# Block-sparse attention and a residual MLP on one core: the first head's keys prepared in two pieces

## The chip, the core and the metric

The kernel runs on one core of a Trainium2 chip. The core has five engines with instruction queues of their own, which work side by side and wait for each other through semaphores: PE (TensorE, matrix products; its weight loads are listed as PEld), DVE (VectorE), ACT (ScalarE), POOL (GpSimd) and SP (SyncE). The last two mainly issue transfers (DMA) here. PE reads the on-chip memory and writes to PSUM, eight banks of 512 float32 values per partition; DVE and ACT read PSUM and write back to the on-chip memory, which has 128 partitions.

The metric is device microseconds of one launch. The kernel before takes 306.7 us (median of six runs, 305.7 to 308.58).

## The reference

Two stages are chained. The first is attention with a block mask, for 4 batches, 8 heads, 768 positions and 64 numbers per head:

```python
scores = scale * np.matmul(q, k.transpose(0, 1, 3, 2))
mask = np.abs(blk_i - blk_j) <= window          # 24 blocks of 32 positions
mask = mask | (blk_i == 0) | (blk_j == 0) | (blk_i == n_blocks - 1) | (blk_j == n_blocks - 1)
for qb in range(n_blocks):
    for kb in sampled_blocks[qb]:               # 3 sampled blocks per row of blocks
        mask[qb*block:(qb+1)*block, kb*block:(kb+1)*block] = True
scores = np.where(mask, scores, -1000000000.0)
attn = softmax(scores)
x = matmul(attn, v)                             # then (batch, seq, 512)
```

The second stage is a residual MLP that also mixes positions:

```python
a1 = alpha1 * x + beta1
u = x + lam * np.einsum('ts,bsd->btd', w_tok, a1)
a2 = alpha2 * u + beta2
out = u + lam * (np.maximum(a2 @ w_ch1, 0.0) @ w_ch2)
```

## The kernel before

**Units.** The 32 heads are worked in 16 pairs (4 batches of 4 pairs). Each pair needs 9 units of 1024 score columns, so there are 144 units. A unit is: scores on PE (L922 for the first six pairs, L941 after them) into a PSUM tile `sps` or into two banks `gb`; an exponential on ACT (L960) into a buffer `eT`; and products with v on PE (L984). A column of ones beside v in `vext` gives the sum of the row, by which DVE divides (L1000, L1003). For the first six pairs the mask is part of the score product: the transposed keys carry 24 more rows that say to which block a position belongs, the queries 24 rows with -400 where a block is masked. For later pairs DVE multiplies by a mask (L965).

**Getting q and k into place.** The score product needs q and k with the head's numbers on the partitions. For the first six pairs PE transposes 128x128 tiles against an identity (L425), three of q and three of k per head, and DVE or ACT copies the result out of PSUM into `qk` (L481), 64 partitions at a time, so there are two copies (r = 0 and 1) per transposed bank. Later pairs use transposing DMAs on SP's queue (L818, L841) and two copying DMAs (L862).

**The MLP.** Per pair or two pairs, DVE makes `a1p` (L1156, L1167), PE multiplies by the transposed token weights `wtokT` (L1205), DVE adds into `x_sb` (L1229) and makes `ub` (L1243). Per half batch follow 16 products with the first channel weights (L1352) with a ReLU on ACT or DVE (L1391, L1399), and the second channel weights (L1432) with the final sum (L1454) and the output DMA (L1473).

**What sets the order.** Two parts. A hand-written start, up to L458, puts the first instructions on each engine in program order. It is the part that the change edits: on SP's queue the load of the first head's q (`q2f`, L360), three loads of the block rows, the second head's q (L365); on ACT's queue the sampled blocks (L359) and the two heads of k (`k2f`, L361, L364); on POOL counters, then loads. DVE builds the mask rows and the identity, PE makes two small products (L430) that say which blocks are masked, ACT and DVE cast q and k to bf16 (`first_cast`, into `relp`), PE transposes three tiles of each, and DVE copies q's, ACT k's. `keep_warm` issues products of constants into a bank that nobody reads.

After it comes a planner, `Plan`. Every later instruction group is an operation with the engines that may run it, an estimated duration, a due time, the operations that it depends on, and the PSUM banks or buffers that it needs. `Plan.run` steps through an estimated time and gives each engine that is free the ready operation with the earliest due time, so the order on every engine, and whether DVE or ACT makes a copy, come out of these estimates; it is written down as program order. Three of its inputs are touched by the change: the estimated time at which each engine is free after the start (the second dictionary given to `Plan`, L463), the estimated landing of the second head's q and k (L892), and `SEEDS` (L48). For each seed a part of the due times within a stretch of the schedule is shifted at random, with the same outcome in each build. Twenty-four single constant products (`fill`, L686) have the latest due times of all, so they stand wherever the planner sees PE with nothing else to do, and the rest of them at the end.

The loads of q, k, v and weights go out on POOL's queue, in an order that the planner also sets. With eight semaphores, a load waits for the one eight places before it.

Of the kernel before, what the change touches and what calls it, by code (L numbers as in the profile page):

```python
# [24 lines left out]
D = 64  # L25
# [5 lines left out]
P = 128  # L31
NT = S // P
HS = S // 2
# [11 lines left out]
EXPB = -0.35667494  # L45
T0 = 6
FINE = 3
SEEDS = [3340310007, 3340310011, 3340310015, 3340310024, 3340310026, 3340310027, 3340310065, 3340310070, 3340310081, 3340310120, 3340310138, 3340310152, 3340310166, 3340310177, 3340310178, 3340310179, 3340310340, 3340310371, 3340310405, 3340310518, 3340310537, 3340310574, 3340310590, 3340310686, 3340310729, 1340310788, 1340310806, 1340310822, 1340310954, 1340310957, 3340311162, 3340311192, 3340311406, 3340311549, 3340312202, 3340312526, 3340312534, 1340312821, 1340312995, 2340313211, 2340313318, 1340313338, 3340313793, 1340314038, 1340314057, 1340314590, 1340315664, 3340316245, 1363480032, 1363480039, 3363480372, 3363480518, 1363480765, 4363481891, 4363482185, 4363482912, 4363483188]  # L48
NFILL = 24
ORD = ((0, 2, 4, 1, 3, 5), (1, 3, 5, 0, 2, 4))  # L50
HF = 3 * S
# [222 lines left out]
def kernel(  # L274
# [17 lines left out]
    nc = tc.nc  # L292
# [21 lines left out]
    qkr = [t[0:D].rearrange("p w h (g r t) -> p w h g r t", g=3, r=2) for t in qk2]  # L314
# [17 lines left out]
    relp = pp.tile([P, 2, 2, NT * D], BF, name="relp", tag="relp")  # L332
# [18 lines left out]
    gbT = [ps.tile([P, 512], FP, name=f"gb{i}", tag=f"gb{i}") for i in range(4)]  # L351
# [6 lines left out]
    k2f = wk.tile([P, 2, NT * D], FP, name="k2f", tag="hts", bufs=2)  # L358
# [33 lines left out]
    def keep_warm(n, w, to=gbT[3]):  # L392
        for _ in range(n):
            nc.tensor.matmul(to[:, 0:w], ones[:, 0:P], ones[:, 0:w], start=True, stop=True)  # L394

    keep_warm(6, 512)

    def where(out, what, op, lim):
        nc.vector.tensor_single_scalar(out, cnt[what][0].bitcast(U16), float(lim), op=op)
# [8 lines left out]
        out=eqt[MB, :, 0:NR],  # L408
# [5 lines left out]
        out=mbb[MB, :], in_=eqt[MB], axis=mybir.AxisListType.X, op=ALU.max  # L414
# [3 lines left out]
    def first_cast(a, i, eng):  # L418
        src = (q2f, k2f)[i]
        eng(out=relp[:, a, i, :], in_=src[:, a, :])  # L420

    def transposes(bank, src, slots=range(NT)):
        tps = bank.bitcast(BF)[:, 0 : NT * P].rearrange("p (o c) -> p o c", o=NT)
        for o in slots:
            nc.tensor.transpose(tps[:, o, :], src(o), identb[:])  # L425
        return tps

    bq_ps = (spsT[1], gbT[2])
    for w in (0, 1):
# [4 lines left out]
            start=True,  # L434
            stop=True,
        )
    first_cast(0, 1, nc.scalar.copy)
    first_cast(0, 0, nc.vector.tensor_copy)
    nc.scalar.activation(
        qx2[0][MB, 0, HS:S], bq_ps[1][0:NBLK, 0:HS], AF.Copy, bias=-BIG, scale=BIG  # L440
# [2 lines left out]
        out=qx2[0][MB, 0, 0:HS],  # L443
# [3 lines left out]
        op0=ALU.mult,  # L447
        op1=ALU.subtract,
    )
    keep_warm(2, P)  # L450
    for w in range(2):
        t = transposes(gbT[w][:], lambda o: relp[:, 0, w, ts(o, P)], range(3))
        for r in range(2):
            cp = nc.scalar.copy if w else nc.vector.tensor_copy
            cp(out=qkr[0][:, w, 0, :, r, :], in_=t[r * D : (r + 1) * D, 0:3])
    keep_warm(10, P)
    for t in vext:
        nc.vector.memset(t[:, :, :, D:VW], 1.0)  # L458


    pl = Plan(
        dict(sps=2, gb=4, eT=NE, q=4, k=4, v=4, vx=3, qk=2, hts=2, a1p=2, ub=2, ot=2),
        dict(PE=5800, ACT=6050, DVE=5800, POOL=4000, SP=4000),  # L463
    )
    GB = [("gb", 0), ("sps", 0)]
    GL = [("gb", 0), ("sps", 0)]
# [71 lines left out]
    def landed(name, t):  # L538
        op = Op(name, [], 0, None)
        op.start, op.vis = 0, t  # L540
        return op
# [88 lines left out]
    for g in range(4):  # L630
# [6 lines left out]
                deps=[x.tr for x in WTT],  # L637
# [31 lines left out]
        deps=[BC["lam"]],  # L669
# [216 lines left out]
    for i in range(2):  # L886
        op = pl.dve(
            ("fc", i),
            dve(384, 2),
            1 + 0.1 * i,  # L890
            lambda op, i=i: first_cast(1, i, nc.vector.tensor_copy),
            deps=[landed(("f", i), 5600 - 500 * i)],  # L892
        )
        FC1.append(op)
    ROWS = []
# [630 lines left out]
```

## Time and profile before

The profiled execution took 306.59 us, of which 304.8 us are the span from the first to the last instruction.

| what | us | where it is from |
|---|---|---|
| profiled execution | 306.59 | times |
| its span | 304.8 | page |
| PE busy | 297.8 (98%) | page, part 1 |
| DVE busy | 232.4 (76%) | page, part 1 |
| ACT busy | 177.4 (58%) | page, part 1 |
| first k, first head landed, cast on ACT begins | 4.45 | order of time, ACT |
| first score product | 6.01 | order of time, PE |
| first exponential | 6.83 | order of time, ACT |
| first product with v | 10.07 | order of time, PE |
| first use of the token weights | 28.36 | order of time, PE |

How to read it: a row in order of time gives the start and the duration in us, the engine, the line, the operation, what it writes and reads with shapes and types, how often it stands in a row, and in brackets how long the engine was idle before it and what ended that. A row of windows gives, for each stretch, its length, the busy time of PE, PEld, DVE, ACT and POOL with the number of instructions, the granted PE clock, the share of the DMA engines in use and what they moved. Products on PE are pipelined: a 512-wide one lasts 0.38 us in the record, but the next starts 0.22 us after it, so pace is read from the distance of the starts. Busy shares over the whole span hide stages: ACT is over nine tenths busy between 10 and 30 us and idle in the last 50.

### The profile page before, as it was taken

What the parts mean: (1) busy time and instruction counts of PE and PEld (TensorE: products, weight loads), DVE (VectorE), ACT (ScalarE), POOL (GpSimd) and SP (SyncE); (2) the same over time, 40 slices, a digit from 0 to 9 for tenths busy, and PEclk for the clock granted to TensorE, in tenths of its full rate; (3) what the DMA queues carried; (4) which work ended last, traced back from release to release, by engine and by line L of the source; (5) the groups of instructions that cost most, each with busy time, mean ns of one, the idle gap of its engine ahead of it and who ended that gap; (6) DMA issues with size and microseconds to landing.
All of it is one profiled execution on the core that took longest, in us unless ns stands there. A gap on an engine that the chain in (4) does not pass through costs nothing.

```text
span 304.8 us, 7147 instructions
## 1 busy us (share of the span) xinstructions
PE 297.8 (98%) x2967; PEld 186.3 (61%) x2996; DVE 232.4 (76%) x438; ACT 177.4 (58%) x242; POOL 44.6 (15%) x71
## 2 busy tenths in 40 slices
PE   7899999999999999999999999999999999999997
PEld 2677888765674566555756565555665574555545
DVE  5669989999799699858977986878778763856532
ACT  5898799988597765768577454767567520000000
POOL 9466252304010102110000000000000000000000
DMA  7999999999967726945161225123030005000011
GB/s 146 205 251 200 206 205 206 199 153 135 180 109 117 131 54 93 178 85 115 38 115 39 76 62 103 38 62 87 2 86 37 0 2 150 8 34 34 37 65 72
DMA packets 50672, 31.38 MB, mean 103 GB/s; under 512 B 27784, under 2 KB 47056, under 8 KB 50640
## 3 DMA queue, kind: packets, MB, share of 16 engines
q0 software_dynamic: 17520, 15.47, 33.4%
q1 hardware_dynamic: 32796, 15.06, 21.8%
q8 instruction: 23, 0.38, 0.5%
q10 hardware_dynamic: 324, 0.39, 0.4%
q14 instruction: 9, 0.07, 0.1%
HBM read 30.78 MB, written 6.29 MB: 122 GB/s over the span
## 4 chain that ended last, share of the span: by engine, by line
PE 90%; ACT 5%; DMA 2%; issue 2%; DVE 1%; SPq 0%; ACTq 0%
PE gb L1352 27%; PE gb L1432 27%; PE gb L984 11%; PE gb L1205 10%; PE sps L922 5%; ACT eT L960 4%; PE sps L941 4%; PE gb L941 3%; DMA q2f<-in_q_dram 2%; PE gb L425 1%; PE sps L1205 0%; SPq L363 0%; PE gb L394 0%; DVE qk L899 0%; ACT wtokT L479 0%
## 5 line engine op out<-in xcount | busy, mean ns | idle before, releaser
L960 ACT ACTIVATE eT<-sps 128x1024 f16<-128x1024 f32 x114 | 110.8, 1033 | 6.3 <-PE sps L922 5.4
L1352 PE MATMUL gb<-uT,w1b 128*128 128x384 bf16 (+1 forms) x508 | 92.3, 326 | 0.0
L1432 PE MATMUL gb<-w2b,hts 128*128 128x512 bf16 (+2 forms) x371 | 88.4, 370 | 1.6 <-issue 0.2
L1352 PEld LDWEIGHTS <-w1b 128*128 128x128 bf16 x512 | 48.1, 98 | 33.0 <-issue 1.2
L965 DVE TENSOR_TENSOR eT<-eT,msk 128x1024 f16<-128x1024 f16 x90 | 58.8, 684 | 9.7 <-ACT eT L960 9.7
L1432 PEld LDWEIGHTS <-hts 128*128 128x128 bf16 x400 | 35.9, 98 | 36.9 <-issue 3.2
L984 PEld LDWEIGHTS <-eT 128*128 128x128 f16 x1152 | 47.7, 97 | 16.3 <-issue 4.9
L1399 DVE TENSOR_SCALAR hts<-gb,b1t 128x384 bf16<-128x384 f32 x72 | 44.2, 616 | 15.8 <-PE gb L1352 14.1
L960 ACT ACTIVATE eT<-gb 128x512 f16<-128x512 f32 x60 | 32.5, 594 | 40.1 <-PE gb L941 40.1
L984 PE MATMUL gb<-vext,eT 128*128 128x65 f16 x1152 | 52.8, 193 | 1.2 <-DVE vext L1022 1.1
L1391 ACT ACTIVATE hts<-gb,b1t 128x384 bf16<-128x384 f32 x55 | 31.8, 585 | 16.5 <-PE gb L1352 14.1
L1205 PE MATMUL gb<-a1p,wtokT 128*128 128x256 bf16 (+1 forms) x348 | 34.2, 250 | 0.0
L1205 PEld LDWEIGHTS <-wtokT 128*128 128x128 bf16 x360 | 29.3, 98 | 5.9 <-issue 1.6
L922 PE MATMUL sps<-qk 88*128 88x512 bf16 (+1 forms) x144 | 31.6, 325 | 0.8
L1454 DVE TENSOR_TENSOR ot<-x_sb,gb 128x512 f32<-128x512 f32 (+2 forms) x25 | 16.6, 663 | 16.2 <-PE gb L1432 15.8
L1229 DVE TENSOR_TENSOR x_sb<-x_sb,gb 128x512 f32<-128x512 f32 (+1 forms) x25 | 15.9, 642 | 5.8 <-PE gb L1205 5.6
L1003 DVE TENSOR_TENSOR x_sb<-gb,rcp 128x384 f32<-128x384 f32 x32 | 17.8, 557 | 1.1
L941 PE MATMUL sps<-qk 64*128 64x256 bf16 x180 | 17.9, 305 | 0.0
L941 PEld LDWEIGHTS <-qk 64*128 64x128 bf16 x240 | 9.3, 94 | 12.7 <-issue 8.4
L1243 DVE TENSOR_TENSOR ub<-x_sb,a_bc 128x512 bf16<-128x512 f32 (+1 forms) x26 | 16.3, 645 | 0.4
L550 POOL DMA_DIRECT2D v<-in_v_dram x15 | 10.6, 707 | 36.3 <-DVE vext L1022 24.8
L1167 DVE TENSOR_TENSOR a1p<-a1p,b_bc 128x768 bf16<-128x768 bf16 (+1 forms) x17 | 15.4, 905 | 0.2
(74 smaller groups left out, 164.0 us busy)
## 6 DMA issues: line engine op xcount, KB each, us to landing
out_dram<-ot SPq DMA_DIRECT2D x23, 256.0 KB, 2.0
v<-in_v_dram POOLq DMA_DIRECT2D x16, 192.0 KB, 7.7
q<-in_q_dram POOLq DMA_DIRECT2D x15, 192.0 KB, 7.8
k<-in_k_dram POOLq DMA_DIRECT2D x15, 192.0 KB, 7.9
w1b<-in_moe_w_ch_dram POOLq DMA_DIRECT2D x4, 512.0 KB, 11.5
w2b<-in_moe_w_ch_dram POOLq DMA_DIRECT2D x4, 512.0 KB, 13.0
qk<-qk SPq DMA_DIRECT2D x20, 96.0 KB, 4.1
wtk<-in_moe_w_tok_dram POOLq DMA_DIRECT2D x3, 384.0 KB, 8.7
```

Source lines behind the costliest of these rows:

```text
L922: nc.tensor.matmul(spsT[sl(key[0])][:, o : o + w], kx2[i][0:KC, a, ts(jt, P)], qx2[i][0:KC, a, c : c + w], start=True, stop=True,)
L941: nc.tensor.matmul(half(key, r)[:, o : o + w], kd[i][rows, h, g, :], qx2[i][rows, h, c : c + w], start=True, stop=True,)
L960: nc.scalar.activation(out_, in_, AF.Exp, bias=EXPB, scale=SCALE)
L965: nc.vector.tensor_tensor(out=e, in0=e, in1=msk[:, :, x : x + 512], op=ALU.mult)
L984: nc.tensor.matmul(bk[:, t * VW : t * VW + D + 1], eTt[sl(("eT", i))][:, ts(col, P)], vx[:, a, jt, 0 : D + 1], start=(r == 0), stop=(r >= ...
L1003: nc.vector.tensor_tensor(out=x_sb[:, s0 : s0 + NT, h * D : (h + 1) * D], in0=o[:, :, 0:D], in1=rc[:].unsqueeze(2).broadcast_to([P, NT, D] ...
L1205: nc.tensor.matmul(bank(bk)[:, j * wp * P : (j + 1) * wp * P], wtokT[:, s, ts(m * g + j, P)], a1p[sl(ak)][:, s, 0:wp, :].rearrange("p w c ...
L1352: nc.tensor.matmul(bank(bk)[:, 0 : HS + w0], w1b[:, dk, ts(f, P)], rhs[dk], start=(dk == 0), stop=(dk == 3),)
L1391: nc.scalar.activation(htsT[hk][:, f, :], bank(bk)[:, w0 : HS + w0], AF.Relu, bias=b1t[:, f : f + 1], scale=1.0,)
L1399: nc.vector.tensor_scalar(out=htsT[hk][:, f, :], in0=bank(bk)[:, w0 : HS + w0], scalar1=b1t[:, f : f + 1], scalar2=0.0, op0=ALU.add, op1=A ...
L1432: nc.tensor.matmul(bank(ck)[:, cs], htsT[hk][:, nk, ts(mt, P)], w2h["t"][:, nk, cs], start=(nk == 0), stop=(nk == 15),)
L1454: nc.vector.tensor_tensor(out=ot[sl(okey)][:, cs], in0=x_sb[:, b % NXB * NT + t, cs], in1=bank(ck)[:, cs], op=ALU.add,)
```

## The change

The keys of the first head are handled in two pieces. The first third (128 of the 384 columns, two of the six tiles of 128 positions) is cast by ACT, transposed into a bank of its own and copied out by ACT; the other two thirds are cast by DVE, transposed into a third bank (`gbT[2]`, which held a mask product until ACT had read it) and copied out by DVE. ACT's copy of the mask rows now stands ahead of its cast of the keys instead of after it, and ACT's wide cast is gone. The products of constants are placed anew: one after the six wide ones, three ahead of the transposes (two before), three after them (ten before). The planner's estimates of when PE, ACT and DVE are free after the start are raised, to 5950, 6100 and 6300 ns from 5800, 6050 and 5800, and the second head's q and k are now said to land at 7000 and 6800 ns (5600 and 5100 before). Ten seeds are added to the list, which shift some due times once more.

So the order of everything after the start is planned again. The hand-written part and the estimates are these:

```diff
-SEEDS = [ ..., 4363482912, 4363483188]
+SEEDS = [ ..., 4363482912, 4363483188, 1382590026, 4382590413, 4382590423, 4382590431, 2382580781, 1382591202, 2382582015, 2382583582, 4382594112, 1382594473]
...
     keep_warm(6, 512)
+    keep_warm(1, P)
...
-    first_cast(0, 1, nc.scalar.copy)
     first_cast(0, 0, nc.vector.tensor_copy)
     nc.scalar.activation(
         qx2[0][MB, 0, HS:S], bq_ps[1][0:NBLK, 0:HS], AF.Copy, bias=-BIG, scale=BIG
     )
...
-    keep_warm(2, P)
-    for w in range(2):
-        t = transposes(gbT[w][:], lambda o: relp[:, 0, w, ts(o, P)], range(3))
+    nc.scalar.copy(out=relp[:, 0, 1, 0:P], in_=k2f[:, 0, 0:P])
+    nc.vector.tensor_copy(out=relp[:, 0, 1, P:HS], in_=k2f[:, 0, P:HS])
+    keep_warm(3, P)
+
+    for w, bk, o0, o1, cp in (
+        (0, gbT[0], 0, 3, nc.vector.tensor_copy),
+        (1, gbT[1], 0, 1, nc.scalar.copy),
+        (1, gbT[2], 1, 3, nc.vector.tensor_copy),
+    ):
+        t = transposes(bk[:], lambda o: relp[:, 0, w, ts(o, P)], range(o0, o1))
         for r in range(2):
-            cp = nc.scalar.copy if w else nc.vector.tensor_copy
-            cp(out=qkr[0][:, w, 0, :, r, :], in_=t[r * D : (r + 1) * D, 0:3])
-    keep_warm(10, P)
+            cp(out=qkr[0][:, w, 0, o0:o1, r, :], in_=t[r * D : (r + 1) * D, o0:o1])
+    keep_warm(3, P)
...
-        dict(PE=5800, ACT=6050, DVE=5800, POOL=4000, SP=4000),
+        dict(PE=5950, ACT=6100, DVE=6300, POOL=4000, SP=4000),
...
-            deps=[landed(("f", i), 5600 - 500 * i)],
+            deps=[landed(("f", i), 7000 - 200 * i)],
```

In the order that results, DVE and PE differ mainly in the first 60 us. Around the second head DVE's order before was: cast of q, cast of k, three row copies, the small be2 cast, first copy of the transposed head, copy of v, second copy. It is now: two row copies, cast of k, cast of q, the third row copy, copy of v, the be2 cast, both copies of the transposed head. On PE the scores of the third unit now stand between the transposes of the second head's q and k, and six of the 24 single constant products ahead of them. Of the copies that either engine may make, one of the six of `wtokT` and two of `qk` go from ACT to DVE, and one of `uT` from DVE to ACT. SP's order is unchanged; on POOL's queue a few loads change places.

## The prediction

> **What bounds the kernel now.** I read the page's first two parts, then windows of the span, then the waits of PE, then ACT and DVE in order of time over the first 17 us.
>
> The first line of the page, and a table by windows (busy time of each engine, granted clock, DMA share, GB/s):
>
> ```profile
> PE 297.8 (98%) x2967; PEld 186.3 (61%) x2996; DVE 232.4 (76%) x438; ACT 177.4 (58%) x242; POOL 44.6 (15%) x71
> ```
>
> ```profile
> 0.00:10.00 10.00, 7.17 (x43) 3.06 (x44) 6.50 (x23) 6.18 (x8) 8.23 (x19) 1.00 0.79 158
> 10.00:30.00 20.00, 19.37 (x295) 15.26 (x295) 14.43 (x30) 18.45 (x20) 11.97 (x18) 1.00 1.21 222
> 30.00:60.00 30.00, 29.80 (x472) 24.00 (x470) 28.10 (x62) 26.88 (x32) 11.12 (x17) 1.00 1.27 204
> 60.00:150.00 90.00, 89.40 (x890) 54.87 (x900) 77.31 (x149) 64.31 (x93) 13.28 (x19) 1.00 0.74 116
> 150.00:290.00 140.00, 138.84 (x1188) 81.64 (x1203) 101.94 (x171) 61.54 (x90) 0.00 (x0) 1.00 0.23 55
> ```
>
> See in them: PE is the bound nearly everywhere, and of its idle time 2.83 us lie in the first 10 us, where the change is made. From 30 us on it misses under 1% of each window. So what PE gains before 30 us should reach the end, unless something else fills it. Busy time overstates PE: against each width's usual spacing after 30 us (0.216 us at 512 columns, 0.109 at 256, 0.056 at 128), the starts of its products lose 4.9 us in the first 10 us, 2.0 between 10 and 30, 1.1 between 30 and 60, and nothing after that.
>
> The waits of PE (total us, times, longest):
>
> ```profile
> PE gb L984 <- DVE vext L1022: 1.1, 1, 1.1
> ...
> PE gb L425 <- DVE relp L420: 0.5, 1, 0.5
> PE gb L425 <- ACT relp L420: 0.4, 1, 0.4
> ```
>
> ACT, then DVE, in order of time (start, us, instruction, idle before it):
>
> ```profile
> 4.45 0.51 ACT L420 CAST relp<-k2f 128x384 bf16<-128x384 f32 x1 [0.90 <-DMA k2f<-in_k_dram]
> 4.98 0.48 ACT L439 ACTIVATE qk<-gb 24x384 bf16<-24x384 f32 x1
> 5.49 0.97 ACT L455 COPY qk<-gb 64x384 bf16<-64x384 bf16 x2
> 6.83 1.94 ACT L960 ACTIVATE eT<-sps 128x1024 f16<-128x1024 f32 x2 [0.37 <-PE sps L922]
> 8.96 1.02 ACT L960 ACTIVATE eT<-sps 128x1024 f16<-128x1024 f32 x1 [0.19 <-PE sps L922]
> 10.95 5.66 ACT L960 ACTIVATE eT<-sps 128x1024 f16<-128x1024 f32 x6 [0.96 <-PE sps L922]
> ```
>
> ```profile
> 7.29 0.43 DVE L420 CAST relp<-q2f 128x384 bf16<-128x384 f32 x1 [1.84 <-DMA q2f<-in_q_dram]
> 7.64 0.34 DVE L420 CAST relp<-k2f 128x384 bf16<-128x384 f32 x1
> 8.01 0.95 DVE L899 COPY qk<-qk 24x768 bf16<-24x768 bf16 x3
> 8.99 0.18 DVE L660 CAST uT<-be2T 128x4 bf16<-128x4 f32 x1
> 9.20 0.55 DVE L481 COPY qk<-gb 64x768 bf16<-64x768 bf16 x1
> 9.67 0.34 DVE L1022 COPY vext<-v 128x768 f16<-128x768 f16 x1
> ```
>
> See: ACT does four things in a row (4.45 to 6.46) before the scores can start. DVE waits 1.84 us for the second head's q, then does three row copies and others before it copies v at 9.67, for which PE waits 1.08 us. The first v had landed at 8.58, q's second half at 7.27, k's at 6.82 (landing events).
>
> **The change, part by part.** All sums are against the profiled execution: 306.59 us, a span of 304.8 and 1.8 around it, 0.1 under the shown median of 306.7.
>
> *Constant products.* One 128-wide product more before the mask products, three before the transposes for two, three after them for ten. The first six end near 3.29 and the mask product waited for DVE until 3.43, so the added one (0.11 at the early rate) is covered by that wait. The third costs 0.06 ahead of q's transposes, whose copies wait longer for DVE anyway. Seven fewer afterwards stood in a gap. Zero; with no cover 0.1 to 0.2.
>
> *First head's k.* ACT now takes the mask half first: its input was there at 4.22, so 4.25 to 4.74 in the time it had idled for k. Then a 128-wide cast and two 64x128 copies replace widths of 384. The trace has none; neighbours are 0.512 and 0.474 at 384, and ACT's exponentials (0.594 at 512, 1.033 at 1024) give 0.86 ns a column, hence 0.29 and 0.26. Cast 4.75 to 5.05, transposes 5.09 to 5.21, copies 5.36 to 5.88; the third score product, the one that needs the second copy, at about 5.92 where it was 6.51, and the first exponential at 6.25 instead of 6.83. Ends: at the widths' full price nothing is gained; at 0.25 each, 0.6. I take 0.58, by the slope. DVE pays 256-wide: cast about 0.28 (0.342 at 384, 0.41 at 512), two copies about 0.29 (0.354 at 384). They delay q's copies from 4.63 to 4.86 and finish near 6.2, inside DVE's 1.84 us wait; two row copies (0.32 each) fill the rest.
>
> *Second head.* The planner is now told that q and k land at 7.0 and 6.8 (before: 5.6 and 5.1), so k is cast first and v's copy moves ahead of the be2 cast and both head copies. DVE: k 6.97, q 7.32, last row 7.69, then v when it has landed, 8.60 to 8.94. PE's first value product starts at 8.98 instead of 10.07: 1.09 us earlier. Nothing but the landing limits it, so that is the upper end; the lower is 0, if v lands as late as it was used. I take 1.09. Queued behind the wait for v are the be2 cast (used far later) and the head copies, now 9.18 to 10.2 where they ended at 10.61; the score product that reads them comes near 10.34, so they hide. The scores of unit 2 now stand ahead of k's transposes, so the third exponential starts near 8.45 (8.96), the fourth near 9.86 (10.95).
>
> *Loads.* The same loads, one reordering that matters early: a small broadcast moves ahead of the third pair's q on POOL's queue, which costs that q at most one small load (0.68 between landings). PE reads it near 21 and it would land at 19.95. SP's order is unchanged. But the first weight block landed at 10.56, and PE used it at 11.69; now it asks at about 10.58. No slack is left there: a late landing costs its whole delay, up to the gain.
>
> *The plan behind.* The new order holds the same 2,954 real products; 304 places differ, none after the 1,050th (85.8 us before). From there both run the same sequence. In 10 to 30 us ACT is the next bound: from 16.92 exponentials follow each other 0.92 apart, with one weight copy between (20.55 to 21.23). That copy goes to DVE, which had a 2.0 us hole near 21, so the saving lies between 0 and 0.68; ACT also waits 0.41 before the tenth exponential. DVE, busy without a break from 22.5 to 39.5, allows about 1.8 in all, since it enters that stretch earlier with one copy more done. I take 0.5 more of this. From 30 to 60 us two copies leave ACT (1.36) and one comes (0.68); DVE takes a net 0.5. PE idles 0.2 there by the table, so between +1.0 (DVE's two added copies in full) and -0.7 (ACT's net) I take 0.
>
> *Sum.* 1.09 + 0.5 = 1.6 earlier, carried to the end: 306.6 - 1.6 = 305.0. The 0.58 of the first exponential is not added, since the third waits on q's landing either way.
>
> *Clock.* In the trace, six 512-wide products take 2.72 us, 0.43 apart, and the same width costs 0.215 later, though the granted clock reads 1.00 throughout; products are fast from about 4.2, and after the 1.08 us wait they still are. So I cost fewer constant products at nothing.
> The Trainium skill, page "TensorE: Matmul & The Clock Gate", section "Part 1: The HAM clock gate", speaks against this: it says full clock is granted only after a window of about 3.4 us of sustained work, free-running, so that the moment varies, and is lost after an idle one. By it the thinner work from 4 to 6 us could leave PE at half rate for one window more, until about 7.5; the first exponential would come some 0.5 later, and the sum would stay at 1.6, as that time is spent waiting for q; no run here shows it yet.
>
> **The rivals.** *Loads hold it back.* PE arrives earlier at loads whose times are set by a queue 1.2 to 1.3 busy until 60 us. The first weights have no slack, pair 6's swapped queries landed at 71.43 and are used at 72.84. Against: no wait of PE for a load is in the list, and pair 6's transposes are issued when PE frees their buffer, so they move with it. Price: the gain clipped to 0.3 to 1.2, about 305.8.
> *More is gained.* ACT's net three copies fewer come to use, and both ACT-bound stretches shorten: up to 1.3 more than my sum, 303.7. For it: exponentials without a gap from 16.92 to 29.7. Against: DVE's 28.10 of 30.
> *Slower: half clock.* If PE falls back to half rate once it works densely, each us of work costs 0.5. The whole gain is gone after 3.2 us at half rate (306.6), and it is slower by 0.5% after 6.3 us, near 308.2. For it: seven products fewer. Against: the longest new idle, 6.75 to 7.70, is shorter than the present 1.08 us that did no harm.
> *It doesn't do what it says.* If the narrow copies cost like wide ones, the first exponential stays at 6.83; the v copy's gain is untouched, so 305.2.
>
> **How the numbers follow.** 0.5%, 1.5 us, is about what a measurement of this kernel can tell from no change. The forecast (1.1 to 2.1 gained; own range 304.5 to 305.5), with the last rival in it: 0.50, three in five of it past 1.5. More gained: 0.18, faster. Loads: 0.18, same. The slower one, with other new waits from the 304 changed places: 0.14, most of it slower. That gives faster 0.50, same 0.38, slower 0.12. The range 303.3 to 307.2 leaves out the far ends of the gain and most of the slow case.
>
> **What would show it.** Right: the mask half ahead of k's cast on ACT, first exponential near 6.25, v's copy near 8.6 with its wait on the load, PE's value products from 9.0, the fourth exponential near 9.9, the tenth near 15.6. PE's waits list loses the 1.1 us line. Wrong: 512-wide scores 0.43 apart after 6 us, a wait of PE for a weight load near 10.6, or idle of PE beyond 0.2 between 30 and 60 us. It fails most likely if DVE, not ACT, sets the pace from 22 to 44 us.

## The result and the profile after

The changed kernel takes 306.26 us (median of 35 runs, 305.52 to 306.9), the kernel before beside it 306.61 (71 runs, 305.37 to 308.58). The ratio is 0.9982, with an interval of 0.9973 to 0.9991: 0.3 to 0.8 us were gained. That is 0.55 us by the ratio and 0.35 between the medians, a third or less of the 1.6 forecast, and less than the 0.5% that was set as the bound. The profiled execution took 306.65 us with a span of 304.9, which is at the upper end of its runs and no shorter than the one of before (306.59, 304.8). So the traces are not compared by their ends alone; below they are compared along the way.

The first line of the page of the changed kernel, then its windows:

```profile
PE 299.8 (98%) x2962; PEld 187.7 (62%) x2991; DVE 234.9 (77%) x443; ACT 175.8 (58%) x240; POOL 44.7 (15%) x71
```

```profile
0.00:10.00 10.00, 9.08 (x51) 4.81 (x52) 7.48 (x26) 4.96 (x8) 8.10 (x19) 1.00 0.78 157
10.00:30.00 20.00, 19.67 (x299) 15.14 (x298) 15.92 (x33) 19.44 (x21) 10.49 (x16) 1.00 1.20 216
30.00:60.00 30.00, 29.84 (x462) 23.84 (x459) 28.31 (x61) 25.57 (x30) 12.22 (x18) 1.00 1.26 204
60.00:150.00 90.00, 89.40 (x888) 55.04 (x897) 77.06 (x149) 64.24 (x93) 13.85 (x20) 1.00 0.75 118
150.00:290.00 140.00, 138.85 (x1190) 81.65 (x1205) 101.93 (x171) 61.54 (x90) 0.00 (x0) 1.00 0.23 55
```

PE is 1.9 us busier in the first window than before, but on 51 products instead of 43, so part of this is products that take longer. ACT is busy 19.44 of the 20 us from 10 to 30 (18.45 before): the exponentials now stand there without a gap. The waits of PE (total, times, longest) have lost the line of 1.1 us:

```profile
PE gb L394 <- PEq L1516: 0.8, 1, 0.8
PE gb L1438 <- issue: 0.2, 1, 0.2
```

Then PE, ACT and DVE of the changed kernel in order of time (start, us, instruction, idle before it):

```profile
5.91 1.86 PE L928 MATMUL sps<-qk 88*128 88x512 bf16 x5
...
8.53 0.99 PE L928 MATMUL sps<-qk 88*128 88x256 bf16 x3
```

```profile
4.38 0.48 ACT L439 ACTIVATE qk<-gb 24x384 bf16<-24x384 f32 x1 [0.84 <-PE gb L431]
4.89 0.30 ACT L450 CAST relp<-k2f 128x128 bf16<-128x128 f32 x1
5.56 0.55 ACT L461 COPY qk<-gb 64x128 bf16<-64x128 bf16 x2 [0.38 <-PE gb L426]
6.96 1.94 ACT L966 ACTIVATE eT<-sps 128x1024 f16<-128x1024 f32 x2 [0.85 <-PE sps L928]
```

```profile
7.31 0.41 DVE L421 CAST relp<-k2f 128x384 bf16<-128x384 f32 x1
7.64 0.34 DVE L421 CAST relp<-q2f 128x384 bf16<-128x384 f32 x1
8.01 0.42 DVE L905 COPY qk<-qk 24x768 bf16<-24x768 bf16 x1
9.12 0.36 DVE L1028 COPY vext<-v 128x768 f16<-128x768 f16 x1 [0.69 <-DMA v<-in_v_dram]
```

The reader is to see two things. The copy of v stands where the forecast put it, ahead of the be2 cast and waiting for the load alone; but v landed at 9.10 in this execution instead of 8.58, so PE's first product with v starts at 9.53, not at the 8.98 of the forecast. And the five score products at 5.91 take 1.86 us where the profile of before had 1.21: PE runs at half rate until about 9.3.

**How the two are compared along the way.** At every point where both kernels have executed the same set of products, the start of the next product is compared with that in the first profile of before. Minus is ahead. The table has all profiles of this study. "Full rate" is the moment from which 128-wide products take 0.22 us in the record instead of 0.31; single matmul records can be missing, so a value stands to about 0.1.

| kernel | order behind the start | full rate from | v lands | first product with v | shift at 10 us | at 28 | at 54 | from 76 on |
|---|---|---|---|---|---|---|---|---|
| before | old | 4.1 | 8.58 | 10.07 | 0 | 0 | 0 | 0 |
| before_again | old | 9.2 | 9.10 | 10.29 | +0.22 | +0.22 | +0.22 | +0.22 |
| nobc_before | old | 3.9 | 8.86 | 9.54 | -0.53 | -0.53 | -0.52 | -0.53 |
| start_new | old | 4.8 | 8.89 | 9.54 | -0.53 | -0.53 | -0.52 | -0.08 |
| start_swapdve | old | 4.7 | 8.74 | 9.18 | -0.89 | -0.90 | -0.88 | -0.17 |
| start_fill_swapdve | old | 6.4 | 8.58 | 9.29 | -0.77 | -0.78 | -0.65 | -0.12 |
| after | new | 9.3 | 9.10 | 9.53 | -0.54 | -1.05 | -0.09 | +0.06 |
| after_again | new | 4.0 | 8.57 | 9.00 | -1.07 | -1.35 | -0.21 | -0.21 |
| after_timed | new | 9.9 | 8.13 | 9.70 | -0.37 | -0.94 | -0.03 | -0.03 |
| plan_new | new | 4.2 | 8.35 | 8.79 | -1.28 | -1.59 | -0.49 | -0.49 |
| fill4 | new | 5.0 | 8.73 | 9.17 | -0.90 | -1.60 | -0.72 | -0.46 |
| q_first | new | 8.6 | 9.06 | 9.50 | -0.57 | -0.80 | -0.10 | -0.11 |
| warm10 | new | 9.6 | 8.51 | 10.02 | -0.05 | -0.56 | +0.12 | +0.95 |
| cold0 | new | 9.7 | 7.97 | 9.63 | -0.44 | -0.81 | +0.29 | +0.29 |
| nobc_after | new | 8.9 | 8.58 | 9.73 | -0.34 | +0.60 | +1.30 | +1.30 |
| seeds_old | no added seeds | 9.1 | 9.13 | 9.57 | -0.50 | -0.27 | +1.2 to +2.1 | +2.5, +3.46 from 100 |

In both old and new order nothing moves after 77 us; what is left there is what the profiled execution's time shows, to within 0.13 us. A profile is one execution and need not stand for the median: that of warm10 took 307.54 us (median 306.59), that of plan_new 306.12 (306.36), that of fill4 306.14 (306.5).

nobc_after took 309.65 us (ratio 1.0086, 1.0054 to 1.0117) and nobc_before 310.29 (1.0072, 1.0038 to 1.0106). The two kernels without broadcast loads ran their other executions 1.4 to 5.5 us longer than the profiled ones, in nobc_before nearly always at a granted clock of 0.989 to 0.994, which is not explained here; they are read from their profiled executions (spans of 306.1 and 304.3 us) and not from their medians.

### The profile page after: what moved, and what is told of

Same layout as the page of the kernel before. It is cut to its first block, busy times and chain, and to the rows that moved or that the text cites. A ratio compares the mean times of both kernels' runs of the same rounds, so it can differ in the third digit from the quotient of the medians.

```text
span 304.9 us, 7142 instructions
## 1 busy us (share of the span) xinstructions
PE 299.8 (98%) x2962; PEld 187.7 (62%) x2991; DVE 234.9 (77%) x443; ACT 175.8 (58%) x240; POOL 44.7 (15%) x71
## 4 chain that ended last, share of the span: by engine, by line
PE 87%; DMA 7%; ACT 2%; POOL 2%; issue 1%; DVE 0%; POOLq 0%; ACTq 0%
PE gb L1358 27%; PE gb L1438 27%; PE gb L1211 10%; PE gb L990 10%; PE sps L947 4%; DMA v<-in_v_dram 4%; PE sps L928 3%; PE gb L947 3%; DMA q<-in_q_dram 3%; ACT eT L966 2%; PE gb L426 1%; POOL wtk L578 1%; POOL k L556 0%; PE sps L1211 0%; POOL wtokT L378 0%
## 5 line engine op out<-in xcount | busy, mean ns | idle before, releaser
L928 PE MATMUL sps<-qk 88*128 88x512 bf16 (+1 forms) x144 | 32.8, 335 | 0.3
L947 PE MATMUL sps<-qk 64*128 64x256 bf16 (+1 forms) x180 | 18.1, 305 | 0.0
L947 PEld LDWEIGHTS <-qk 64*128 64x128 bf16 x240 | 9.4, 94 | 12.5 <-issue 8.2
L556 POOL DMA_DIRECT2D q<-in_q_dram x15 | 10.6, 705 | 36.2 <-DMA qk<-q 28.8
L928 PEld LDWEIGHTS <-qk 88*128 88x128 bf16 x144 | 12.3, 99 | 5.3 <-issue 0.7
```

What stands on the lines that cost most here:

```text
L928: nc.tensor.matmul(spsT[sl(key[0])][:, o : o + w], kx2[i][0:KC, a, ts(jt, P)], qx2[i][0:KC, a, c : c + w], start=True, stop=True,)
L947: nc.tensor.matmul(half(key, r)[:, o : o + w], kd[i][rows, h, g, :], qx2[i][rows, h, c : c + w], start=True, stop=True,)
```

## The experiments

### The start alone and the plan alone

start_new has the new hand-written start and the old seeds and estimates, so the order behind the start is that of before. plan_new has the old start, with its ten constant products, and the new seeds and estimates.

```diff
# start_new, against the changed kernel
-SEEDS = [ ..., 4363483188, 1382590026, ..., 1382594473]
+SEEDS = [ ..., 4363483188]
...
-        dict(PE=5950, ACT=6100, DVE=6300, POOL=4000, SP=4000),
+        dict(PE=5800, ACT=6050, DVE=5800, POOL=4000, SP=4000),
...
-            deps=[landed(("f", i), 7000 - 200 * i)],
+            deps=[landed(("f", i), 5600 - 500 * i)],
# plan_new: these lines as in the changed kernel, all other lines as before
```

> The new hand-written start with the old plan (old seeds, old free times, old landing times), so that everything after the start stands in the order of before. Theory O (the new order behind the start decides): v's copy keeps its old place behind the first head copy, PE's first product with v comes at 9.8 to 10.1, and the time is that of before, 306.6 +- 0.2. Theory L (loads set the pace from about 28 us on): the same, 306.6. Theory C (fewer constant products leave PE at half clock until about 9.3 us, which costs the gain): 306.7 to 307.2, scores 0.43 apart at 6 us.

> The old hand-written start, with ten constant products after the transposes, and the new plan (new seeds, free times and landing times). Theory O: all of the gain is the new order, so the time is that of the changed kernel, 306.2 +- 0.2, with PE's first product with v at 9.0 to 9.5. Theory L: the same, 306.3. Theory C: PE is at full clock at 6 us, so it is faster than the changed kernel, 305.8 or less.

start_new: 306.55 us, ratio 1.0008 (0.9981 to 1.0035). plan_new: 306.36, ratio 0.9995 (0.9978 to 1.0012). Neither alone can be told from before, nor from the changed kernel. But their shifts differ in kind. In start_new the lead of 0.53 us stands unchanged from 10 to 72 us and then loses 0.44 at one spot. In plan_new it is 1.28 at 10 us, grows to 1.59 and falls to 0.49 by 54. So the old order carries a lead from 10 to 72 us, and the loss between 28 and 54 us comes with the new order, whatever the start. One reason for plan_new's big lead is that v landed at 8.35 there.

That the hand-written start gave start_new its 0.53 us is not shown. nobc_before (below) does what the kernel before does on every engine until its first product with v, and it has the same lead of 0.53. In both, the second head's q landed early (6.57 and 6.63, against 7.27 in the first profile of before), and v's copy came at the same time. DVE of nobc_before, where the first profile of before has this copy at 9.67:

```profile
9.14 0.34 DVE L1022 COPY vext<-v 128x768 f16<-128x768 f16 x1
```

### The added seeds

seeds_old is the changed kernel without the ten added seeds.

```diff
-SEEDS = [ ..., 4363483188, 1382590026, ..., 1382594473]
+SEEDS = [ ..., 4363483188]
```

> The changed kernel without the ten added seeds; start, free times and landing times are the new ones. The order is then planned a third way. Theory O: the order matters by some tenths, so it differs from the changed kernel by more than 0.3, more likely slower (306.6 to 307.2). Theory L: loads set the pace whatever the order, within 0.2 of the changed kernel, 306.1 to 306.5. Theory C: the same as the changed kernel, with scores at half clock at 6 us.

309.84 us, ratio 1.0103 (1.0084 to 1.0122). It is level with the changed kernel at 10 us (-0.50), and the rest is lost by the order: 1.4 us between 28 and 42, 0.9 between 42 and 60, 1.2 between 71 and 90. Its windows (as above):

```profile
30.00:60.00 30.00, 28.98 (x454) 23.12 (x452) 26.45 (x55) 25.86 (x29) 10.90 (x16) 1.00 1.26 202
```

PE misses 1.0 of 30 us where the changed kernel misses 0.16. The start and the estimates alone would have made the kernel 1% slower; the added seeds choose an order that takes about 3.5 us back.

### Constant products and the clock

warm10 has ten products after the transposes instead of three. fill4 puts four more between q's transposes and k's, where PE stands idle in the changed kernel until ACT has cast. cold0 has none ahead of the plan. before_again and after_again are the two kernels unchanged, profiled once more.

```diff
# warm10
-    keep_warm(3, P)
+    keep_warm(10, P)
     for t in vext:
# fill4, inside the loop over the three groups of transposes
+        if w == 1 and o0 == 0:
+            keep_warm(4, P)
         t = transposes(bk[:], lambda o: relp[:, 0, w, ts(o, P)], range(o0, o1))
# cold0
-    keep_warm(6, 512)
-    keep_warm(1, P)
...
-    keep_warm(3, P)
...
-    keep_warm(3, P)
```

> The changed kernel with ten constant products after the transposes again instead of three; nothing else differs. Theory C: full clock from 6 us on, third exponential near 8.5 instead of 9.56, 305.8 or less. Theories O and L: within 0.2 of the changed kernel, 306.1 to 306.5, since PE's first product with v waits for the load of v either way; if the products run at half clock they push the first scores back by up to 0.7, hidden by the wait for the second head's q.

> The changed kernel with four more narrow constant products between q's three transposes and k's three, where PE stands idle from 4.9 to 5.24 us until ACT has cast k's first third. Theory A, the gap: TensorE ran at half clock until 9.2 us in the changed kernel, and until 9.5 with ten products put behind the transposes, because this gap breaks an otherwise closed stretch of work; with it closed the clock is up by 6.2 us, the first exponential starts at 6.4 to 6.6 instead of 6.96, PE's first product with v at the landing of v plus 0.45 us, and the end is 0.2 to 0.5 us earlier if the start counts (305.8 to 306.1), or the same (306.2) if later places take it. Theory B, chance: the moment at which the clock goes up differs from one execution to the next whatever the gaps are; then the product durations go to 0.22 us at any time between 4 and 10 us and the time is as the changed kernel's, 306.1 to 306.4.

> The kernel before, unchanged, profiled a second time. If the early loads of its first profile (v at 8.58 us, q of the fourth pair at 25.15, against 8.35 to 9.13 and 26.3 to 28.7 in five kernels since) belong to its order of the loads, they come again within 0.3 us; if they are this execution's chance, q of the fourth pair lands at 26 to 28.5 here and the lead of the loads over the changed kernel is mostly gone. Its clock: up by 4.2 us again if that belongs to the kernel, at another time, up to 9.5 us, if it is chance. Time 306.4 to 306.8.

> The changed kernel, unchanged, profiled a second time. If the loss behind 28 us belongs to its order of the work, PE stands 1.1 to 1.7 us ahead of the kernel before at 27 us (by the landing of v and the clock), gives back 0.8 to 1.0 us by 54 us as in four profiles with this order, and another 0 to 0.3 near 73 us: 305.9 to 306.7. If it is chance, the loss between 28 and 54 us is below 0.4 us in this profile. The clock of TensorE: full from 9 us again if the gap at 4.9 to 5.24 us decides it, at another time from 3.4 us on if it is chance.

> The changed kernel without the constant products ahead of the plan (seven before the mask products, three and three around the transposes; those that the plan places in gaps later stay). If they are what brings TensorE to full clock early, products stay at 0.31 us for 128 columns until 10 us or later, the narrow transposes, the five 512-wide score products and the first products with v all take about twice their time (1.2 us more up to 10 us), and the time is 306.8 to 307.8. If the half clock up to 9 us costs nothing because the landing of v sets the first product with it, 306.1 to 306.4, as with them. If the clock goes up at a time of its own whatever TensorE has done, the same 306.1 to 306.4, with full clock at a time between 3.4 and 9.5 us.

warm10: 306.59 us, ratio 1.0002 (0.9989 to 1.0015). fill4: 306.5, ratio 0.999 (0.997 to 1.001). cold0: 307.25, ratio 1.0018 (0.9993 to 1.0042). before_again 306.85 and after_again 306.4, one run each.

PE of after_again, then of before_again, in order of time:

```profile
5.83 1.03 PE L928 MATMUL sps<-qk 88*128 88x512 bf16 x5 [0.17 <-ACT qk L461]
...
9.00 0.41 PE L990 MATMUL gb<-vext,eT 128*128 128x65 f16 x8
```

```profile
6.56 1.91 PE L922 MATMUL sps<-qk 88*128 88x512 bf16 x5
...
10.29 0.37 PE L984 MATMUL gb<-vext,eT 128*128 128x65 f16 x7 [0.48 <-DVE vext L1022]
```

The same five score products take 1.86 us in one execution of the changed kernel and 1.03 in another, 1.21 in one of before and 1.91 in another. So the moment of full rate belongs to the execution, not to the kernel: 4.1 and 9.2 us for before, 9.3, 4.0 and 9.9 for the changed one. More products in warm10 only put the scores back (first exponential at 7.70, as at 7.66 in before_again, which also has ten of them at half rate, against 6.96 with three) and left the rate at half until 9.6 (first product with v at 10.02, 1.5 us after v landed). With fill4 the rate was full from 5.0, but the same four products in start_fill_swapdve left it at half until 6.4, so it isn't shown that the gap matters. This agrees with the Trainium skill, page "TensorE: Matmul & The Clock Gate", section "Part 1: The HAM clock gate", as far as it says that the observed window runs freely and the moment varies; a spread of 5 us is more than the half microsecond either way that it gives.

cold0 has no constant products before 4 us and full rate only from 9.7. Its first product with v comes 1.66 us after v landed; its profile ends 0.23 behind that of the changed kernel and its median is 0.7 above that of before beside it, but its interval holds 1. So the constant products may be worth up to about 1 us together, or nothing: a moment of full rate as late as 9.7 also came with them (9.9 in after_timed). What their new places are worth at the end, these runs can't tell.

### The late loads

nobc_after and nobc_before leave out the four broadcast loads that stand on POOL's queue between 9 and 18 us; a memset of ones takes the place of each.

```diff
-            nc.gpsimd.dma_start(t[:], src.unsqueeze(0).to_broadcast([P, DM]))
+            nc.gpsimd.memset(t[:], 1.0)
```

> The changed kernel without the four broadcast loads of lam, alpha1, beta1 and alpha2 (each is a memset on POOL instead, so those four vectors are not read; the order of PE, ACT, DVE and SP is the same). Theory 1, late loads: the stream of loads, which is 0.5 us later than before from v on and 2.5 us later from slot 15 on, takes the gain away at two places, 28.5 us (PE waits 0.63 us for q of the fourth pair) and 72.8 us (the half-scores of the seventh pair wait for the second swap, which lands at 72.86). With four loads fewer the stream runs 1 to 3 us ahead, q of the fourth pair lands before 27.5, the swap before 72.3, and PE is ahead of the kernel before by 0.5 to 1.0 us at 75 us: 305.3 to 305.8 us. Theory 2, order of the work: the gain is lost to the new order between 28 and 54 us on PE, ACT and DVE, whatever the loads do: 306.1 to 306.4, the same as the changed kernel.

> The kernel before with the same four loads left out (memsets instead). Its profile shows one late load only (v, ahead of the first product with it, which these four loads come behind). Theory 1, late loads: its PE waits for no load later on, so 306.3 to 306.6, unchanged; the two kernels without broadcast loads stand 0.6 to 1.1 us apart. Theory 2, order of the work: unchanged as well, 306.4 to 306.6, and the two stand 0.2 to 0.5 us apart, as they do with the loads. Above 306.8 or below 306.0 would say that the memsets or the earlier loads do something that neither theory has.

The expected times can't be compared, as said above, but the profiles answer. nobc_after lost 1.6 us at 11 us to something that no theory had: DVE ran beside the memsets. DVE there, in order of time:

```profile
8.82 0.86 DVE L1028 COPY vext<-v 128x768 f16<-128x768 f16 x1
9.60 1.94 DVE L666 CAST uT<-be2T 128x4 bf16<-128x4 f32 x1
11.57 1.14 DVE L487 COPY qk<-gb 64x768 bf16<-64x768 bf16 x2
```

The cast of four columns takes 1.94 us instead of 0.17, and the head copies that PE waits for come behind it. It ends at 11.54, when the two memsets beside it and the load that POOL issues behind them (10.82 to 11.53) are through, so the share of the memsets alone isn't separated. In nobc_before only a head copy out of PSUM falls beside a memset, it takes 0.56 us as usual, and the lead stays.

Behind that, two readings hold. With the broadcast loads gone q of the fourth pair lands at 22.0 instead of 28.5, PE waits for no load, and nobc_after still loses 0.70 us between 28 and 54. So late loads aren't the main cause there. And the second swap of the seventh pair lands at 68.1 and 68.4 us, against 71.0 to 73.7 in the kernels with all loads and the swap at this place: that points to the loads that share the DMA engines. nobc_before and start_new come to it with the same order and the same lead, 0.53 us; the first loses nothing, the second 0.44.

### The gate at 72 us

The half-scores of the seventh pair (L947, L941 before) need both swapped halves. For the second swap, its landing, the time at which PE came to it, and the loss there:

| kernel | swap lands | PE comes | loss |
|---|---|---|---|
| nobc_after | 68.12 | 74.14 | 0 |
| nobc_before | 68.38 | 72.3 | 0 |
| after_timed | 70.98 | 72.81 | 0 |
| q_first | 70.98 | 72.74 | 0 |
| before_again | 71.31 | 73.06 | 0 |
| before | 71.43 | 72.84 | 0 |
| plan_new | 71.62 | 72.35 | 0 |
| after_again | 71.83 | 72.63 | 0 |
| fill4 | 72.33 | 72.12 | 0.26 |
| cold0 | 72.6 | 73.13 | 0 |
| start_new | 72.72 | 72.32 | 0.44 |
| after | 72.86 | 72.75 | 0.15 |
| warm10 | 73.74 | 72.96 | 0.83 |

PE of start_new, then of plan_new, then the waits of PE in warm10:

```profile
72.32 0.83 PE L947 MATMUL gb<-qk 64*128 64x512 bf16 x2
```

```profile
72.35 0.39 PE L941 MATMUL gb<-qk 64*128 64x512 bf16 x2
```

```profile
PE gb L947 <- DMA qk<-qk: 0.4, 1, 0.4
```

Wherever the swap lands after PE has come, there is a loss, and wherever it lands before, there is none. To take the gate away, start_swapdve makes these two swaps copies on DVE in start_new; start_fill_swapdve adds the four products of fill4.

```diff
-                move = nc.sync.dma_start if op.eng == "SP" else nc.vector.tensor_copy
+                move = nc.sync.dma_start if op.eng == "SP" and pi != 6 else nc.vector.tensor_copy
```

> start_new (the new start, the order of before) with one more edit: the two swaps of the seventh pair, which went by DMA, are two copies on DVE at the same place of the emission. Theory 1, the gate: start_new kept its lead of 0.53 us over before to 72.3 us and lost 0.44 there, because the second swap's DMA landed at 72.72, behind the loads that share the DMA engines; without that DMA the lead of 0.5 us (at a landing of v near 8.9) is held to the end, no product of the seventh pair's half-scores waits beyond 0.1 us near 72.5, and the time is 0.3 to 0.5 us below start_new's, 306.0 to 306.3. Theory 2, DVE: DVE is busy 24.0 of 25 us between 55 and 80 in the changed kernel, so two copies of about 0.35 us each delay the copies and affine steps behind them and PE waits elsewhere, +0.3 to +0.7: 306.6 to 307.2. Theory 3, chance: the 0.44 us is this one execution's; no difference to start_new, 306.4 to 306.7.

> The same with four narrow constant products between q's and k's transposes as in fill4. Theory A, the gap: the clock of TensorE is up by 5.5 us, as in fill4 (4.99), the first exponential starts by 6.6 us, the first product with v at v's landing plus 0.4 to 0.7. Theory B, chance: the clock goes up at any time from 3.4 to 9.5 us. With the gate gone and the order of before, a lead at the start is carried whole, 1 for 1, to the end: at the same landing of v this kernel stands within 0.2 us of start_swapdve where v's copy sets the start, 306.0 to 306.3, and below it by up to 0.4 where the clock does. If the order of before does not carry a lead either, 306.4 to 306.7.

start_swapdve: 307.5 us, ratio 1.0048 (1.0022 to 1.0075). start_fill_swapdve: 307.27, ratio 1.0029 (1.0007 to 1.005). The wait at 72 us is gone in both, and a lead of 0.65 to 0.9 us is carried to 66 us; there 0.72 and 0.53 are lost, five us earlier than before. DVE, then PE of start_swapdve:

```profile
65.21 0.35 DVE L868 COPY qk<-qk 64x768 bf16<-64x768 bf16 x1
65.58 0.65 DVE L741 COPY msk<-some 128x576 f16<-128x576 f16 x1
66.25 0.35 DVE L868 COPY qk<-qk 64x768 bf16<-64x768 bf16 x1
```

```profile
66.10 0.82 PE L1358 MATMUL gb<-uT,w1b 128*128 128x385 bf16 x4
67.47 0.82 PE L1358 MATMUL gb<-uT,w1b 128*128 128x385 bf16 x4 [0.55 <-DMA q<-in_q_dram]
```

The two copies took 0.7 us of an engine that is busy 9.57 of the 10 us from 60 to 70 in start_new, and PE waits about as long for a bank that DVE empties late (the profile names a load that had long landed; in start_fill_swapdve it names DVE). So in these profiles taking the gate away moved the loss to DVE. The medians lie 1.0 and 0.7 us above these two executions (306.54 and 306.6); why is not shown.

### Two loads exchanged

In four profiles with the new order (after, after_again, cold0, fill4) PE waits 0.23 to 0.48 us for q of the fourth pair near 28.4 us. q_first gives that load the place ahead of its k, which it has in the kernel before; the orders of PE, ACT, DVE and SP are unchanged. after_timed is the changed kernel, timed beside it.

```diff
+    due = {op.name: op for op in pl.ops if op.name[0] in ("load", "bc")}
+    due["load", "q", 3].due = due["load", "k", 3].due - 0.5
     pl.run()
```

> The changed kernel with two loads in exchanged order: q of the fourth pair ahead of its k, as the kernel before has them; PE, ACT, DVE and SP keep their order. Theory 1, the late load is worth its wait: q lands about 0.5 to 1.1 us earlier (27.3 to 27.9), the wait of 0.24 to 0.48 us ahead of its transposes near 28.4 is gone, and as PE is the fullest engine from 28 us on this reaches the end: 0.2 to 0.5 us below the changed kernel beside it, 305.8 to 306.1. Theory 2, the exponentials take it: what is saved at 28.4 is lost again by the waits for ACT between 39 and 54 us, so that the shift of PE behind 54 us is the same: no difference beyond 0.15 us. k of the fourth pair lands 0.5 us later, near 28.5; its transposes at 33.4 are not reached by that.

> The changed kernel, unchanged, timed on the same chip as q_first. 306.1 to 306.4, ratio to before 0.997 to 1.000. In its profile PE stands 0.7 to 1.4 us ahead of the kernel before at 27 us, depending on when v lands, and gives back 0.7 to 1.15 us by 54 us, of it 0.24 to 0.48 at 28.4 in a wait for q of the fourth pair.

q_first: 306.39 us, ratio 0.9986 (0.997 to 1.0002). after_timed: 306.3, ratio 0.9976 (0.9952 to 1.0). The wait at 28.4 is gone, but so it is in after_timed, where that q landed at 27.95 without the exchange. And q of the third pair was late in the profiled execution of q_first, so its lead at 28 us is smaller (0.80). From there it still loses 0.70 by 54 us, as nobc_after does, and stands where the changed kernel stands. The exchange is worth nothing that can be measured.

## Why the prediction was wrong in its size

**The start: right in its mechanism, but the term of 1.09 is about twice too large.** From v's landing to the first product with it the kernel before took 1.49 and 1.19 us, the changed one 0.43 in two of its three profiles (the third is told below). But the forecast took two landings of one profile as fixed. v landed anywhere from 7.97 to 9.13 us in the sixteen profiles. And in the old order v's copy starts 2.4 to 2.9 us after the second head's q has landed, which was at 7.27 in the first profile of before and at 6.13 to 6.76 in the other five with that order; in nobc_before, with q at 6.63, the 1.49 was 0.68. An estimate from the column at 10 us: the start of before has 0, +0.22 and -0.53 there (the last from nobc_before), the changed kernel -0.54, -1.07 and -0.37, which is 0.56 apart on average.

**The narrow operations: right on ACT, not on DVE.** The narrow cast took 0.30 and the two copies 0.26 each (forecast 0.29 and 0.26). At full rate the first exponential starts at 6.46 instead of 6.83, 0.37 gained (forecast 0.58). At half rate it is 6.96 instead of 7.66, but warm10 at 7.70 shows that there the seven constant products fewer make this difference, which the forecast put at zero. DVE's cast of 256 columns took 0.51 (0.28); q's copies stand behind it, and PE's first score product (5.91) starts when they end (5.86).

**Clock costed at nothing: wrong as an assumption.** It costs nothing when v is late (9.10 in the first profile after). In after_timed v landed at 8.13 and the first product with v came at 9.70, behind transposes and scores at half rate: 1.1 us of the lead there. What the Trainium skill says about the varying moment, weighed in the prediction and then left out of the sum, belonged into it.

**ACT's copy: right in size.** "I take 0.5": between 10 and 28 us the changed kernel gains 0.51, 0.28 and 0.57 in its three profiles, fill4 0.70. Between 19.8 and 25.4 us, where the copy stood on ACT, the gain is 0.58 or 0.59 in all profiles with the new order but q_first, where a late load takes part of it. The forecast of the lead at 28 us was 1.6; it measured 1.05, 1.35 and 0.94.

**The step that failed is "From 30 to 60 us ... between +1.0 and -0.7 I take 0", and with it "carried to the end"; the 1.09, of which about 0.56 was there, is the second.** In nine profiles with the new order 0.68 to 1.14 us are lost between 28 and 54 us (1.10 in plan_new, 0.96 in the profile after), in the five with the old order none but 0.13 in one. Of this, 0.26 to 0.73 goes between 28 and 32 us and 0.39 to 0.66 after 32. The true value was near the upper bound, and not for the reason given for that bound: of PE's waits from 27 to 54 us in the profile after, DVE ends only one (0.13). ACT in order of time, before and then after:

```profile
37.62 2.86 ACT L960 ACTIVATE eT<-sps 128x1024 f16<-128x1024 f32 x3 [0.24 <-PE gb L1205]
40.81 1.94 ACT L960 ACTIVATE eT<-sps 128x1024 f16<-128x1024 f32 x2 [0.34 <-PE sps L922]
42.77 0.80 ACT L479 COPY qk<-gb 64x768 bf16<-64x768 bf16 x1
43.59 1.94 ACT L960 ACTIVATE eT<-sps 128x1024 f16<-128x1024 f32 x2
```

```profile
38.36 3.77 ACT L966 ACTIVATE eT<-sps 128x1024 f16<-128x1024 f32 x4 [0.38 <-PE gb L426]
42.16 0.80 ACT L485 COPY qk<-gb 64x768 bf16<-64x768 bf16 x1
42.98 2.85 ACT L966 ACTIVATE eT<-sps 128x1024 f16<-128x1024 f32 x3
46.42 1.02 ACT L966 ACTIVATE eT<-sps 128x1024 f16<-128x1024 f32 x1 [0.59 <-PE sps L928]
```

Then PE of the changed kernel:

```profile
39.44 0.59 PE L928 MATMUL sps<-qk 88*128 88x512 bf16 x3
...
40.35 0.59 PE L928 MATMUL sps<-qk 88*128 88x512 bf16 x2
...
41.27 0.42 PE L990 MATMUL gb<-vext,eT 128*128 128x65 f16 x8
...
44.05 0.59 PE L928 MATMUL sps<-qk 88*128 88x512 bf16 x2
```

From 38.4 to 45.8 us ACT now works without a break, and PE's scores come as fast as ACT frees their banks: the exponentials end at 39.38, 40.30, 41.22, 42.13 and 44.00, and 0.05 us after each of these PE starts a product that its semaphores tie to that exponential (39.44, 40.35, 41.27, 42.18 and 44.05). Between the same two points of work (39.46 to 45.95 before, 38.67 to 45.72 after) PE's starts lose 0.16 us beyond their usual distance in one place before, 0.74 in these five places after, four ahead of a score product and one ahead of a product with v. All nine profiles with the new order have these five waits, 0.72 to 0.75 us together, and lose 0.54 to 0.56 between the two points, whether PE comes there 1.40 us ahead of before (fill4) or 0.60 behind (nobc_after). So it is not that a fixed moment cuts the lead off: the new order itself costs this time. To be set against it is one wait of 0.31 us for an exponential at 38.69 in the kernel before, which the changed kernel doesn't have. Between 27 and 32 us the changed kernel's starts lose 0.19 for scores and 0.30 for q of the fourth pair, at 53.7 another 0.13. These are waits of 0.07 to 0.30 us, and the list of PE's waits of this profile, which the forecast read for the kernel before, shows none of them. No run took the waits in the forties away alone.

**The rival that came nearest is "Loads hold it back"**, 305.8 with the gain clipped to 0.3 to 1.2. It named the two places where a load does count: the first weight block (in after_again PE waits 0.2 us for it) and the swap of the seventh pair. It dismissed the second because PE's buffer release would move it along; it does, but the time from issue to landing was 4.7 us in the first profile of before and 4.3 to 7.8 in the others with all loads, and that spread decides. "More gained" needed the lead to be kept behind 28 us, which no profile with the new order shows. "Half clock" came true as a state: PE ran at half rate until 9.3 us, not for 3 us of dense work later. Its price was paid at the start, where v was early (after_timed, above), and not shown at the end: after_timed ends 0.03 us ahead of before.

**The signs that were named.** The mask half stands ahead of the cast on ACT (4.38), v's copy waits for the load alone, the 1.1 us line is gone, and the fourth exponential starts at 10.48, at full rate (after_again) at 9.88 (forecast near 9.9). The tenth came at 16.45 and 16.15, not near 15.6 (16.92 before). Of the signs against it, scores 0.43 apart after 6 us were there. In after_again PE also waited for the first weights, at 10.99. Idle of PE in the window from 30 to 60 is 0.16 us, below the 0.2 that was named: busy time counts a product that waits a little as busy, so this sign could not show the loss.

**What stays open.** Which exchange in the new order makes PE wait for ACT's exponentials between 38 and 46 us was not isolated; about 300 places differ, and the ten added seeds, with the raised estimates, produced them. No version was found that beats the changed kernel.

## What to carry to other kernels

A lead at the start is worth what the order behind it leaves of it: where a planner reorders the rest, ask first what the same start gives with the old order, and what the new order gives with the old start. Compare kernels at points of equal work, not by their longest waits: here a microsecond went in gaps of 0.07 to 0.30 us, none of which is in the list of waits of the profile after. And before a start is costed from one profile, take a second one of the unchanged kernel: the landing of the first v, that of the second head's q and the moment of full PE rate moved by up to 1.2, 1.4 and 6 us.

## What the runs showed of the hardware

- PE's rate in the first 10 us is a matter of the execution: full from 3.9 to 5.0 us in seven profiles, from 6.4 in one, and from 8.6 to 9.9 in eight, with the granted clock at 1.00 over the first 10 us in all sixteen. Only the durations of the products show it (0.31 against 0.22 us at 128 columns, 0.63 against 0.38 at 512).
- A memset on POOL (0.55 us for 128x512) can hold DVE: a copy of 768 columns took 0.86 us instead of 0.36, a cast of four columns 1.94 instead of 0.17. The Trainium skill, page "SBUF — State Buffer", section "SBUF: two separate sides", says that the two engines share a port pair that one of them holds for a whole instruction; these rows fit with it; here DVE was held past two memsets and the issue of a load behind them.
- The same 96 KB swap took 3.7 and 4.0 us from issue to landing with four loads fewer on another queue, and 4.3 to 7.8 with them.
